# A layer-norm and MLP kernel: two DMA queues at the start, split transposes, and a new order of block 0's products

## The chip, the cores and the metric

The kernel runs on one core of a Trainium2 chip. The metric is the device time of one execution in microseconds (us). The "span" of a profile is the time from the first to the last instruction of one profiled execution; it is about 1.8 us shorter than that execution's time. PE is the matrix engine (TensorE), DVE is VectorE, ACT is ScalarE, POOL is GpSimd, SP is SyncE, and PEld is PE's loading of weights.

## The reference, cut to what matters

```python
# x: (1, 2048, 1024), w1: (1024, 3584), w2: (3584, 1024), all bf16
y = (x - mean(x)) / sqrt(var(x) + 1e-5)     # per row of 1024
h = gelu(y @ w1 + b1)                       # tanh approximation
out = h @ w2 + b2
```

## The kernel before

The 2048 rows of x are 16 tiles of 128 rows; 4 tiles make a block, so there are 4 blocks. For each block, PE computes the "first product" (`y @ w1`, 28 column blocks called `ft`, each a sum over 8 slices) and then the "second product" (`h @ w2`). All weights stay in SBUF after one load. In blocks 1 to 3 the first product takes all 4 tiles at once, 512 columns per matmul. In block 0 the data is still arriving, so it is cut into rectangles of tiles and `ft`:

```python
# (block, first tile, number of tiles, first ft, last ft)
rects.append((0, 0, 1, 0, lead_ft))                 # tile 0 alone, ft 0..3  (128 columns)
for i in range(1, NH):
    rects.append((0, i, 1, 0, lead_ft))             # tile 1 alone, ft 0..3
rects.append((0, 0, NH, lead_ft, KF))               # tiles 0 and 1, ft 4..27 (256 columns)
rects.append((0, NH, TPB - NH, 0, KF))              # tiles 2 and 3, ft 0..27 (256 columns)
```

The prologue of block 0: SyncE issues all loads in this order.

```python
for t in blocks[0][:NH]:
    load_x(t)                       # tile 0 in two halves, then tile 1
sp.dma_start(b1_raw[:], ...)        # b1
load_w1(0)                          # w1 chunk 0: ft 0..3, 1 MB
load_w1(1)
for t in blocks[0][NH:]:
    load_x(t)                       # tiles 2 and 3
for ci in range(2, NW1C):
    load_w1(ci)
# ... b2, the next block's x, w2, the rest of x
```

VectorE takes statistics of a tile (`st`, twice; `ag`; `ve`), POOL computes 1/sqrt, VectorE normalises (`nm`). PE then transposes the tile in 8 steps, and ScalarE and VectorE each copy half of the result from PSUM to `yT_sb` (`ET`), after all 8 steps. Until then PE runs 16 "warm-up" matmuls on zeros, and it transposes b1 before tile 0:

```python
pe_ops = [("warm", i) for i in range(n_warm)] + [("b1T",)]
pe_ops.append(("T", blocks[0][0]))
...
elif kind == "ET":                                   # on ScalarE
    a.wait_ge(sem_pe, pe_cnt[("T", t)])
```

So the first product needs two things: its weights (w1 chunk 0) and `yT` of tile 0.

Of the kernel before, what the change touches and what calls it, by code (L numbers as in the profile page):

```python
# [10 lines left out]
P = 128  # L11
LN_EPS = 1e-5
BANK = 512
# [10 lines left out]
def _mixer_mlp(nc, x, w1, b1, w2, b2, out, cfg):  # L24
# [7 lines left out]
    TPB = min(cfg.get("tiles_per_block", 4), TT)  # L32
    assert TT % TPB == 0
# [6 lines left out]
    CH = D // NCH  # L40
    W1C = min(cfg.get("w1_chunk", 512), F)
    assert F % W1C == 0 and W1C % P == 0
    NW1C = F // W1C
    FPC = W1C // P
    W2C = min(cfg.get("w2_chunk", 4), KF)
    assert KF % W2C == 0
    NW2C = KF // W2C
    NP1 = cfg.get("p1_banks", 3)
    NP2 = cfg.get("p2_banks", 2)
    NTB = cfg.get("t_banks", 2)  # L50
    assert NP1 + NP2 + NTB + 1 <= 8
    assert KD * P * 2 <= BANK * 4
    n_warm = cfg.get("n_warm", 0)
    tail_split = list(cfg.get("tail_split", [DBS]))
    dma_t = cfg.get("dma_transpose", True) and NB > 1
    lead = cfg.get("lead", True) and TPB >= 2
    lead_ft = min(cfg.get("lead_ft", FPC), KF)
    t1_after = cfg.get("t1_after", 2)
    t_first = cfg.get("t_first", 6)
    t_gap = cfg.get("t_gap", 3)  # L60
    KH = KD // 2 if KD >= 2 else KD
# [7 lines left out]
    NH = min(2, TPB)  # L69

    rects = []
    if lead:
        rects.append((0, 0, 1, 0, lead_ft))
        for i in range(1, NH):
            rects.append((0, i, 1, 0, lead_ft))
        if lead_ft < KF:
            rects.append((0, 0, NH, lead_ft, KF))
    else:
        rects.append((0, 0, NH, 0, KF))
    if TPB > NH:  # L80
        rects.append((0, NH, TPB - NH, 0, KF))
# [10 lines left out]
    def p2_ranges(t):  # L92
# [3 lines left out]
        assert sum(tail_split) == DBS  # L96
# [7 lines left out]
    pe_T_tiles = list(blocks[0]) if dma_t else list(range(TT))  # L104
    split_tiles = set(blocks[0]) if KH < KD else set()

    pe_ops = [("warm", i) for i in range(n_warm)] + [("b1T",)]
    pe_ops.append(("T", blocks[0][0]))
    pend_T = list(blocks[0][1:])
    if not lead:  # L110
        for _ in range(NH - 1):
            pe_ops.append(("T", pend_T.pop(0)))
    for ri in range(first_late_rect):
# [5 lines left out]
        for k, ft in enumerate(range(f0, f1)):  # L119
            pe_ops.append(("P1", ri, ft))  # L120
            done = k + 1
            if lead and ri == 0 and done == min(t1_after, f1 - f0):
                for _ in range(NH - 1):
                    pe_ops.append(("T", pend_T.pop(0)))
            if wide and i0 == 0 and pend_T and done >= t_first and (done - t_first) % t_gap == 0:
                pe_ops.append(("T", pend_T.pop(0)))
# [4 lines left out]
    for b in range(NB):  # L131
# [4 lines left out]
        nxt = list(blocks[b + 1]) if (b + 1 < NB and not dma_t) else []  # L136
        groups = [(t, o, w) for t in blocks[b] for (o, w) in p2_ranges(t)]
        stride = max(1, len(groups) // TPB)
        for gi, (t, o, w) in enumerate(groups):
            pe_ops.append(("P2", t, o, w))  # L140
            if nxt and gi % stride == 0:
                pe_ops.append(("T", nxt.pop(0)))
        for t in nxt:
            pe_ops.append(("T", t))
# [3 lines left out]
    t_seq = [op for op in pe_ops if op[0] == "T"]  # L148
# [8 lines left out]
    rot = {"early": 0, "late": 0}  # L157
    for (_, t) in t_seq:
        early = t in split_tiles
        pool = (T_BANKS + P2_BANKS) if early else T_BANKS  # L160
        key = "early" if early else "late"
        parts = []
        pieces = [(0, KH, "act"), (KH, KD, "dve")] if t in split_tiles else [(0, KD, "act")]
# [493 lines left out]
```

## Time and profile before

| | |
|---|---|
| time, median of 16 runs | 402.16 us (401.51 to 404.93) |
| span of the profiled run | 400.4 us |
| PE busy | 395.7 us, 99% |
| first product starts | 8.94 us |
| w1 chunk 0 complete | 8.80 us |
| yT of tile 0 ready | 8.34 us |
| second product of block 0 starts | 59.64 us |

The page of the profile opens with the span; its part 1 gives the busy time of each engine, its part 4 the chain of work that ended last.

```profile
span 400.4 us, 4765 instructions
PE 395.7 (99%) x2153; PEld 204.7 (51%) x2153; DVE 57.2 (14%) x120; ACT 89.0 (22%) x150; POOL 10.4 (3%) x23
PE 97%; DMA 2%; SPq 0%; issue 0%; DVE 0%
```

PE bounds the kernel and hardly ever waits. Only the time before its first product and the length of its matmul stream can be won. The same chain in order of time (start, length, what) shows both; L585 is the first product, L563 the transposes, L606 the second product.

```profile
1.70 0.42 SPq L341
2.16 0.46 SPq L359
2.67 6.13 DMA w_sb<-in_w_dram
...
8.94 1.05 PE ps L585 x16
...
18.80 1.75 PE ps L585 x16
20.55 0.06 issue
20.61 1.03 PE ps L585 x8
...
22.09 37.55 PE ps L585 x344
59.64 48.35 PE ps L606 x224
```

The issue of x tile 1 (L341) and of b1 (L359) stand before that of w1 chunk 0, whose data is complete at 8.80. At 20.55 there is a small wait. The timeline (start, length, engine, line, operation) shows the other chain, to `yT` of tile 0.

```profile
1.23 5.81 PE L547 MATMUL ps<-zero_sb 128*128 128x512 bf16 x16 [1.23 <-DVE zero_sb L441]
5.52 0.55 DVE L463 TENSOR_SCALAR x_sb<-x_sb,mv,rstd 128x1024 bf16<-128x1024 bf16 x1
7.09 0.62 PE L563 MATMUL ps<-ident,x_sb 128*128 128x128 bf16 x8
7.74 0.60 ACT L510 ACTIVATE yT_sb<-ps 128x512 bf16<-128x512 bf16 x1 [5.47 <-PE ps L563]
7.75 0.42 DVE L474 COPY yT_sb<-ps 128x512 bf16<-128x512 bf16 x1 [0.65 <-PE ps L563]
```

Tile 0 is normalised at 6.07, but the warm-ups hold PE until 7.04. Both copies are done at 8.34, still before the weights. In the view by windows (the last two columns are the share and the rate of the DMA engines, in GB/s) there is a hole in the stream of loads:

```profile
4.00:4.50 0.50, 0.50 (x2) 0.15 (x1) 0.47 (x2) 0.00 (x0) 0.00 (x0) 1.00 0.48 111
4.50:5.00 0.50, 0.50 (x2) 0.15 (x1) 0.47 (x3) 0.00 (x0) 0.07 (x1) 1.00 0.67 137
5.00:5.50 0.50, 0.50 (x3) 0.18 (x2) 0.40 (x1) 0.00 (x0) 0.49 (x1) 1.00 0.99 340
```

Last, the matmuls of the first product by form (count | busy us, mean ns):

```profile
L585 PE MATMUL ps<-yT_sb,w_sb 128*128 128x512 bf16 x672 | 145.5, 379 | 0.0
L585 PE MATMUL ps<-yT_sb,w_sb 128*128 128x256 bf16 x416 | 46.1, 273 | 0.1
```

Matmuls overlap, so the mean of one (273 or 379 ns) is longer than the spacing of the stream, and the rate is read from the chain: 37.55 us / 344 = 109.2 ns per matmul of 256 columns, 48.35 / 224 = 215.8 ns per matmul of 512.

### The profile page before, as it was taken

The page shows a single profiled execution, that of the slowest core. Times are in us where ns is not written, and L with a number is a line of the kernel's source. Part 1 is how long each engine was busy: PE and PEld are TensorE (multiplying, and loading weights), DVE is VectorE, ACT ScalarE, POOL GpSimd, SP SyncE. Part 2 cuts the span into 40 slices and gives each one's busy share as a digit, 9 for nine tenths or more (in the row PEclk, how much of TensorE's full clock was granted, in tenths as well). Part 3 has the DMA queues.
Part 4 walks back from the last instruction along what each step waited for, and adds up shares of the span by engine and source line. Part 5 has one row for each costly group of instructions (what it writes and reads, how often), then busy time and mean ns, then how long its engine had stood idle before and what let it go on. Part 6 is the DMA issues. An engine that isn't in the chain of part 4 may idle for free.

```text
span 400.4 us, 4765 instructions
## 1 busy us (share of the span) xinstructions
PE 395.7 (99%) x2153; PEld 204.7 (51%) x2153; DVE 57.2 (14%) x120; ACT 89.0 (22%) x150; POOL 10.4 (3%) x23
## 2 busy tenths in 40 slices
PE   7999999999999999999999999999999999999997
PEld 3988884444444444444444444444444444444446
DVE  5506100101260000101153000001100000001101
ACT  2655550000034442000013444100003344400000
POOL 1102000000020000000011000000000000000000
PEclk9999999999999999999999999999999999999999
DMA  7999964000014000000003200000000000000000
GB/s 244 354 362 387 386 213 82 26 26 28 21 34 78 0 0 2 5 22 28 26 28 62 43 2 0 0 28 26 0 28 26 2 0 0 2 0 26 28 26 28
DMA packets 29038, 26.79 MB, mean 67 GB/s; under 512 B 13786, under 2 KB 21466, under 8 KB 29018
## 3 DMA queue, kind: packets, MB, share of 16 engines
q1 hardware_dynamic: 29018, 26.49, 21.0%
q8 instruction: 17, 0.28, 0.3%
q14 instruction: 3, 0.02, 0.0%
HBM read 19.14 MB, written 4.19 MB: 58 GB/s over the span
## 4 chain that ended last, share of the span: by engine, by line
PE 97%; DMA 2%; SPq 0%; issue 0%; DVE 0%
PE ps L585 49%; PE ps L606 48%; DMA w_sb<-in_w_dram 2%; PE ps L563 0%; SPq L335 0%; SPq L359 0%; SPq L341 0%; DVE x_sb L484 0%
## 5 line engine op out<-in xcount | busy, mean ns | idle before, releaser
L585 PE MATMUL ps<-yT_sb,w_sb 128*128 128x512 bf16 (+2 forms) x1152 | 195.3, 332 | 1.3 <-DMA w_sb<-in_w_dram 1.2
L606 PE MATMUL ps<-w_sb,hT_sb 128*128 128x512 bf16 (+2 forms) x952 | 194.2, 366 | 0.0
L585 PEld LDWEIGHTS ps<-yT_sb,w_sb 128*128 128x128 bf16 x1152 | 109.8, 98 | 85.6 <-ACT yT_sb L510 1.4
L606 PEld LDWEIGHTS ps<-w_sb,hT_sb 128*128 128x128 bf16 x952 | 90.9, 98 | 102.7
L522 ACT ACTIVATE hT_sb<-ps,b_sb 128x512 bf16<-128x512 f32 (+2 forms) x144 | 85.2, 592 | 255.1 <-PE ps L585 254.8
L484 DVE TENSOR_TENSOR x_sb<-ps,b_bc 128x512 bf16<-128x512 f32 (+2 forms) x34 | 22.4, 660 | 318.3 <-PE ps L606 318.3
L449 DVE BATCH_NORM_STATS2 stats<-x_sb 128x6 f32<-128x512 bf16 x32 | 20.6, 682 | 13.7 <-DMA x_sb<-in_x_dram 13.7
L426 POOL TENSOR_TENSOR rstd<-veps,nhalf 128x1 f32<-128x1 f32 x16 | 9.7, 607 | 201.8 <-DVE veps L457 201.8
L463 DVE TENSOR_SCALAR x_sb<-x_sb,mv,rstd 128x1024 bf16<-128x1024 bf16 x16 | 7.9, 540 | 0.6 <-POOL rstd L426 0.4
L547 PE MATMUL ps<-zero_sb 128*128 128x512 bf16 x16 | 5.8, 544 | 1.2 <-DVE zero_sb L441 1.2
L547 PEld LDWEIGHTS ps<-zero_sb 128*128 128x128 bf16 x16 | 2.0, 133 | 4.5 <-issue 2.9
L510 ACT ACTIVATE yT_sb<-ps 128x512 bf16<-128x512 bf16 x4 | 2.4, 597 | 5.6 <-PE ps L563 5.5
L453 DVE BATCH_NORM_AGGREGATE mv<-stats 128x2 f32<-128x12 f32 x16 | 3.3, 209 | 0.6
L474 DVE COPY yT_sb<-ps 128x512 bf16<-128x512 bf16 x4 | 1.7, 424 | 6.8 <-PE ps L563 6.8
L457 DVE TENSOR_SCALAR veps<-mv 128x1 f32<-128x1 f32 x16 | 2.5, 154 | 0.6
L563 PE MATMUL ps<-ident,x_sb 128*128 128x128 bf16 x32 | 2.5, 219 | 0.0
L563 PEld LDWEIGHTS ps<-ident,x_sb 128*128 128x128 bf16 x32 | 2.0, 98 | 0.1
L503 ACT ACT_TABLE_LOAD x1 | 1.3, 1283 | 0.8 <-PEq L642 0.8
L441 DVE MEMSET zero_sb<- 128x256 uint32 x1 | 0.3, 272 | 0.9 <-PEq L642 0.9
L554 PEld LDWEIGHTS ps<-ident,b_raw 28*128 28x128 bf16 x1 | 0.1, 91 | 0.4 <-issue 0.4
L416 POOL TENSOR_SCALAR_AFFINE_SELECT ident<-ones_sb 128x128 bf16<-128x128 bf16 x1 | 0.3, 292 | 0.1
L413 POOL MEMSET ones_sb<- 128x128 bf16 x1 | 0.2, 204 | 0.3 <-POOLq L642 0.3
(8 smaller groups left out, 1.1 us busy)
## 6 DMA issues: line engine op xcount, KB each, us to landing
w_sb<-in_w_dram SPq DMA_DIRECT2D x14, 1024.0 KB, 13.4
x_sb<-in_x_dram SPq DMA_DIRECT2D x15, 256.0 KB, 8.7
out_dram<-x_sb SPq DMA_DIRECT2D x15, 256.0 KB, 2.0
x_sb<-in_x_dram SPq DMA_DIRECT2D x2, 128.0 KB, 2.3
b_bc<-in_b_dram SPq DMA_DIRECT2D x1, 256.0 KB, 9.5
yT_sb<-x_sb SPq DMA_TRANSPOSE x12, 3.1
out_dram<-x_sb SPq DMA_DIRECT2D x1, 128.0 KB, 1.7
out_dram<-x_sb SPq DMA_DIRECT2D x1, 64.0 KB, 2.7
```

The costliest lines, as they stand in the source:

```text
L426: ins = g.tensor_tensor(out=rstd[:, t:t + 1], in0=veps[:, t:t + 1], in1=nhalf[:], op=ALU.pow)
L449: ins = v.bn_stats(out=stats[:, t, ch, :], in_=x_sb[:, t, ch * CH:(ch + 1) * CH])
L453: ins = v.bn_aggr(out=mv[:, t, :], in_=stats[:, t, :, :].rearrange("p a b -> p (a b)"))
L457: ins = v.tensor_scalar(out=veps[:, t:t + 1], in0=mv[:, t, 1:2], scalar1=LN_EPS, scalar2=None, op0=ALU.add)
L463: ins = v.tensor_scalar(out=x_sb[:, t, :], in0=x_sb[:, t, :], scalar1=mv[:, t, 0:1], scalar2=rstd[:, t:t + 1], op0=ALU.subtract, op1=ALU.mult,
L484: ins = v.tensor_tensor(out=x_sb[:, t, o:o + w], in0=p2_bank(gi % NP2)[:, 0:w], in1=b2_bc[:, o:o + w], op=ALU.add,)
L510: ins = a.activation(out=yT_sb[:, slot, k0:k1, col:col + P], in_=t_part_ap(part).rearrange("p (k n) -> p k n", k=k1 - k0), func=ACTF.Copy,)
L522: ins = a.activation(out=hT_sb[:, ft, i0 * P:(i0 + nt) * P], in_=p1_bank(gi % NP1)[:, 0:nt * P], func=ACTF.Gelu_apprx_tanh, bias=b1_sb[:, ...
L547: ins = pe.matmul(p2_bank(op[1] % NP2), lhsT=zero_sb[:, 0:P], rhs=zero_sb[:], start=True, stop=True,)
L563: ins = pe.transpose(out=t_part_ap(part)[:, (kd - k0) * P:(kd - k0 + 1) * P], in_=x_sb[:, t, kd * P:(kd + 1) * P], identity=ident[:],)
L585: ins = pe.matmul(p1_bank(gi % NP1)[:, 0:nt * P], lhsT=w1_sb[:, kd, ft * P:(ft + 1) * P], rhs=yT_sb[:, slot, kd, i0 * P:(i0 + nt) * P], st ...
L606: ins = pe.matmul(p2_bank(gi % NP2)[:, 0:w], lhsT=hT_sb[:, kf, i * P:(i + 1) * P], rhs=w2_sb[:, kf, o:o + w], start=(kf == 0), stop=(kf == ...
```

## The change

Its intent: get the first product started earlier, and keep PE fed afterwards. It has three parts.

- **D, DMA.** b1 and x tile 1 are issued on ScalarE's queue; on SyncE, w1 chunk 0 follows x tile 0 at once.
- **C, prologue on the engines.** 12 warm-ups instead of 16. b1's transpose comes after tile 0's. 8 small "fill" matmuls follow. Each transpose is two operations of 4 steps (`Ta`, `Tb`), so ScalarE's copy starts after the first.
- **R, order of the products.** Tiles 0 and 1 together only up to `ft` 11, then tiles 2 and 3 up to 11, then all four with 512 columns. Tiles 2 and 3 are transposed earlier, and VectorE's order is adapted.

The diff cut to its core; removed options of the old configuration, renamings and the moved load functions are left out.

```diff
+PAIR_FT = 12
-    t_first = cfg.get("t_first", 6)          # steps before tile 2's transposes
-    t_gap = cfg.get("t_gap", 3)
+T_FIRST = 4
+T_GAP = 2
@@ rects
-            rects.append((0, 0, NH, lead_ft, KF))
-        rects.append((0, NH, TPB - NH, 0, KF))
+        rects.append((0, 0, NH, lead_ft, pair_ft))
+        rects.append((0, NH, TPB - NH, 0, pair_ft))
+            rects.append((0, 0, TPB, pair_ft, KF))
@@ PE's order
-    pe_ops = [("warm", i) for i in range(n_warm)] + [("b1T",)]     # n_warm = 16
-    pe_ops.append(("T", blocks[0][0]))
+    pe_ops = [("warm", i) for i in range(N_WARM)]                  # N_WARM = 12
+    pe_ops.append(("T", blocks[0][0]))
+    pe_ops.append(("b1T",))
+    pe_ops += [("fill", i) for i in range(N_FILL)]                 # N_FILL = 8
...
+    pe_ops = [h for op in pe_ops for h in ([("Ta", op[1]), ("Tb", op[1])] if op[0] == "T" else [op])]
@@ SyncE
-            for t in blocks[0][:NH]:
-                load_x(t)
-            sp.dma_start(b1_raw[:], ...)
-            load_w1(0)
+            load_x(sp, blocks[0][0])
+            load_w1(sp, 0)
@@ ScalarE
+            a.wait_ge(sem_pool, pool_cnt[("ones",)])
+            load_b1(a)
+            load_x(a, blocks[0][1])
...
-                    a.wait_ge(sem_pe, pe_cnt[("T", t)])
+                    a.wait_ge(sem_pe, pe_cnt[("Ta", t)])
```

More of the change, by code (lines that the diff above doesn't have):

```diff
@@ L11 @@
 P = 128
+BANK = 512
 LN_EPS = 1e-5
-BANK = 512
+TILES_PER_BLOCK = 4
+W1_CHUNK_FT = 4
+W2_CHUNK_KT = 4
+NP1 = 3
+NP2 = 2
+NTB = 2
+N_WARM = 12
+N_FILL = 8
+LEAD_FT = 4
+T1_AFTER = 2
+T_FIRST = 4
+T_GAP = 2
+X_AFTER = 2
+PAIR_FT = 12
+TAIL_SPLIT = (256, 128, 128)
 def _number(ops):
@@ L21, in _number, with _mixer_mlp @@
     return res
-def _mixer_mlp(nc, x, w1, b1, w2, b2, out, cfg):
+def _mixer_mlp(nc, x, w1, b1, w2, b2, out):
     xf = x.rearrange("b s d -> (b s) d")
@@ L30, in _mixer_mlp @@
     TT, KD, KF = S // P, D // P, F // P
-    TPB = min(cfg.get("tiles_per_block", 4), TT)
-    assert TT % TPB == 0
+    TPB = min(TILES_PER_BLOCK, TT)
+    assert TT % TPB == 0 and TPB >= 2
     NB = TT // TPB
@@ L40, in _mixer_mlp @@
     CH = D // NCH
-    W1C = min(cfg.get("w1_chunk", 512), F)
-    assert F % W1C == 0 and W1C % P == 0
-    NW1C = F // W1C
-    FPC = W1C // P
-    W2C = min(cfg.get("w2_chunk", 4), KF)
+    assert KD >= 2 and KD * P * 2 <= BANK * 4
+    assert NP1 + NP2 + NTB + 1 <= 8
+    KH = KD // 2
+    NH = 2
+    w1_bounds = [(f0, min(KF, f0 + W1_CHUNK_FT)) for f0 in range(0, KF, W1_CHUNK_FT)]
+    NW1C = len(w1_bounds)
+    w1_chunk_of = {ft: ci for ci, (f0, f1) in enumerate(w1_bounds) for ft in range(f0, f1)}
+    W2C = min(W2_CHUNK_KT, KF)
     assert KF % W2C == 0
     NW2C = KF // W2C
-    NP1 = cfg.get("p1_banks", 3)
-    NP2 = cfg.get("p2_banks", 2)
-    NTB = cfg.get("t_banks", 2)
-    assert NP1 + NP2 + NTB + 1 <= 8
-    assert KD * P * 2 <= BANK * 4
-    n_warm = cfg.get("n_warm", 0)
-    tail_split = list(cfg.get("tail_split", [DBS]))
-    dma_t = cfg.get("dma_transpose", True) and NB > 1
-    lead = cfg.get("lead", True) and TPB >= 2
-    lead_ft = min(cfg.get("lead_ft", FPC), KF)
-    t1_after = cfg.get("t1_after", 2)
-    t_first = cfg.get("t_first", 6)
-    t_gap = cfg.get("t_gap", 3)
-    KH = KD // 2 if KD >= 2 else KD
+    lead_ft = min(LEAD_FT, KF)
+    tail_split = list(TAIL_SPLIT) if sum(TAIL_SPLIT) == DBS else [DBS]
     xv = xf.rearrange("(t p) d -> p t d", p=P)
@@ L68, in _mixer_mlp @@
     blocks = [list(range(b * TPB, (b + 1) * TPB)) for b in range(NB)]
-    NH = min(2, TPB)
-    rects = []
-    if lead:
-        rects.append((0, 0, 1, 0, lead_ft))
-        for i in range(1, NH):
-            rects.append((0, i, 1, 0, lead_ft))
-        if lead_ft < KF:
-            rects.append((0, 0, NH, lead_ft, KF))
-    else:
-        rects.append((0, 0, NH, 0, KF))
+    dma_t = NB > 1
+    pair_ft = KF if TPB <= NH else max(lead_ft, min(PAIR_FT, KF))
+    rects = [(0, 0, 1, 0, lead_ft), (0, 1, 1, 0, lead_ft)]
+    if lead_ft < pair_ft:
+        rects.append((0, 0, NH, lead_ft, pair_ft))
     if TPB > NH:
-        rects.append((0, NH, TPB - NH, 0, KF))
+        rects.append((0, NH, TPB - NH, 0, pair_ft))
+        if pair_ft < KF:
+            rects.append((0, 0, TPB, pair_ft, KF))
     first_late_rect = len(rects)
@@ L95, in p2_ranges @@
             return base
-        assert sum(tail_split) == DBS
         last_o = base[-1][0]
@@ L102, in p2_ranges @@
         return res
-    pe_T_tiles = list(blocks[0]) if dma_t else list(range(TT))
-    split_tiles = set(blocks[0]) if KH < KD else set()
-    pe_ops = [("warm", i) for i in range(n_warm)] + [("b1T",)]
+    split_tiles = set(blocks[0])
+    pe_ops = [("warm", i) for i in range(N_WARM)]
     pe_ops.append(("T", blocks[0][0]))
+    pe_ops.append(("b1T",))
+    pe_ops += [("fill", i) for i in range(N_FILL)]
     pend_T = list(blocks[0][1:])
-    if not lead:
-        for _ in range(NH - 1):
-            pe_ops.append(("T", pend_T.pop(0)))
     for ri in range(first_late_rect):
@@ L121, in _mixer_mlp @@
             done = k + 1
-            if lead and ri == 0 and done == min(t1_after, f1 - f0):
+            if ri == 0 and done == min(T1_AFTER, f1 - f0):
                 for _ in range(NH - 1):
                     pe_ops.append(("T", pend_T.pop(0)))
-            if wide and i0 == 0 and pend_T and done >= t_first and (done - t_first) % t_gap == 0:
+            if wide and i0 == 0 and pend_T and done >= T_FIRST and (done - T_FIRST) % T_GAP == 0:
                 pe_ops.append(("T", pend_T.pop(0)))
@@ L135, in _mixer_mlp @@
                 pe_ops.append(("P1", ri, ft))
-        nxt = list(blocks[b + 1]) if (b + 1 < NB and not dma_t) else []
-        groups = [(t, o, w) for t in blocks[b] for (o, w) in p2_ranges(t)]
-        stride = max(1, len(groups) // TPB)
-        for gi, (t, o, w) in enumerate(groups):
-            pe_ops.append(("P2", t, o, w))
-            if nxt and gi % stride == 0:
-                pe_ops.append(("T", nxt.pop(0)))
-        for t in nxt:
-            pe_ops.append(("T", t))
+        for t in blocks[b]:
+            for (o, w) in p2_ranges(t):
+                pe_ops.append(("P2", t, o, w))
+    pe_ops = [h for op in pe_ops for h in ([("Ta", op[1]), ("Tb", op[1])] if op[0] == "T" else [op])]
     p1_seq = [op for op in pe_ops if op[0] == "P1"]
     p2_seq = [op for op in pe_ops if op[0] == "P2"]
-    t_seq = [op for op in pe_ops if op[0] == "T"]
+    t_seq = [("T", op[1]) for op in pe_ops if op[0] == "Ta"]
     p1_idx = {op: i for i, op in enumerate(p1_seq)}
@@ L156, in _mixer_mlp @@
     bank_user = {}
-    rot = {"early": 0, "late": 0}
+    rot = 0
+    pool_banks = T_BANKS + P2_BANKS
     for (_, t) in t_seq:
-        early = t in split_tiles
-        pool = (T_BANKS + P2_BANKS) if early else T_BANKS
-        key = "early" if early else "late"
         parts = []
-        pieces = [(0, KH, "act"), (KH, KD, "dve")] if t in split_tiles else [(0, KD, "act")]
-        for (k0, k1, eng) in pieces:
-            bank = pool[rot[key] % len(pool)]
-            rot[key] += 1
+        for (k0, k1, eng) in [(0, KH, "act"), (KH, KD, "dve")]:
+            bank = pool_banks[rot % len(pool_banks)]
+            rot += 1
             parts.append((bank, k0, k1, eng))
@@ L174, in _mixer_mlp @@
     for op in pe_ops:
-        if op[0] == "T":
+        if op[0] == "Ta":
             act_ops.append(("ET", op[1]))
@@ L183, in _mixer_mlp @@
     dve_ops = [("zero",)]
-    t0 = blocks[0][0]
-    if lead and NH > 1:
-        t1 = blocks[0][1]
-        h1 = ln_head(t1)
-        dve_ops += ln_head(t0) + h1[:1] + [("nm", t0)] + h1[1:]
-        dve_ops += [("ET", t0)] if t0 in split_tiles else []
-        dve_ops += [("b1c",), ("nm", t1)]
-        dve_ops += [("ET", t1)] if t1 in split_tiles else []
-        rest = blocks[0][2:]
-    else:
-        first = blocks[0][:NH]
-        for t in first:
-            dve_ops += ln_head(t)
-        for t in first:
-            dve_ops.append(("nm", t))
-        dve_ops.append(("b1c",))
-        for t in first:
-            if t in split_tiles:
-                dve_ops.append(("ET", t))
-        rest = blocks[0][NH:]
-    for t in rest:
-        dve_ops += ln_head(t)
+    t0, t1 = blocks[0][0], blocks[0][1]
+    h1 = ln_head(t1)
+    dve_ops += ln_head(t0) + h1[:1] + [("nm", t0)] + h1[1:]
+    dve_ops += [("ET", t0), ("b1c",), ("nm", t1), ("ET", t1)]
+    rest = blocks[0][2:]
+    prev = None
+    for t in rest:
+        h = ln_head(t)
+        if prev is None:
+            dve_ops += h
+        else:
+            dve_ops += h[:1] + [("nm", prev)] + h[1:]
+        prev = t
+    if prev is not None:
+        dve_ops.append(("nm", prev))
     for t in rest:
-        dve_ops.append(("nm", t))
-    for t in rest:
-        if t in split_tiles:
-            dve_ops.append(("ET", t))
+        dve_ops.append(("ET", t))
     for b in range(NB):
@@ L234, in _mixer_mlp @@
         if t == TT - 1 and len(rs) > D // DBS:
-            out_dmas[t] = [(t, o, w, ("E2", t, o, w)) for (o, w) in rs]
+            out_dmas[t] = [(o, w, ("E2", t, o, w)) for (o, w) in rs]
         else:
-            out_dmas[t] = [(t, 0, D, ("E2", t) + rs[-1])]
+            out_dmas[t] = [(0, D, ("E2", t) + rs[-1])]
     dmat_tiles = [t for b in range(1, NB) for t in blocks[b]] if dma_t else []
@@ L324, in wait_yT, with note, load_x @@
             eng.wait_ge(sem_act, act_cnt[("ET", t)])
-            if t in split_tiles:
-                eng.wait_ge(sem_dve, dve_cnt[("ET", t)])
+            eng.wait_ge(sem_dve, dve_cnt[("ET", t)])
+        loads = {}
+        def note(sm, val):
+            loads[sm.name] = (sm, val)
+        def load_x(eng, t):
+            if t == blocks[0][0]:
+                for ch in range(NCH):
+                    eng.dma_start(
+                        x_sb[:, t, ch * CH:(ch + 1) * CH], xv[:, t, ch * CH:(ch + 1) * CH]
+                    ).then_inc(sem_x0[ch], 16)
+                    note(sem_x0[ch], 16)
+                return
+            (sm, val), = x_waits(t, 0)
+            eng.dma_start(x_sb[:, t, :], xv[:, t, :]).then_inc(sm, 16)
+            note(sm, val)
@@ new lines, in load_b1, with load_b2, load_w1 @@
+        def load_b1(eng):
+            eng.dma_start(b1_raw[:], b1.rearrange("(k p) -> k p", p=P)).then_inc(sem_b1, 16)
+            note(sem_b1, 16)
+        def load_b2(eng):
+            eng.dma_start(
+                b2_bc[:], b2.rearrange("(o d) -> o d", o=1).broadcast_to([P, D])
+            ).then_inc(sem_b2, 16)
+            note(sem_b2, 16)
+        def load_w1(eng, ci):
+            f0, f1 = w1_bounds[ci]
+            eng.dma_start(w1_sb[:, :, f0 * P:f1 * P], w1v[:, :, f0 * P:f1 * P]).then_inc(sem_w1[ci], 16)
+            note(sem_w1[ci], 16)
@@ L328, in _, with load_w2 @@
+        def load_w2(eng, ci):
+            eng.dma_start(
+                w2_sb[:, ci * W2C:(ci + 1) * W2C, :], w2v[:, ci * W2C:(ci + 1) * W2C, :]
+            ).then_inc(sem_w2[ci], 16)
+            note(sem_w2[ci], 16)
         @block.sync
         def _(sp):
-            issued = []
-            def load_x(t):
-                if t == blocks[0][0]:
-                    for ch in range(NCH):
-                        sp.dma_start(
-                            x_sb[:, t, ch * CH:(ch + 1) * CH], xv[:, t, ch * CH:(ch + 1) * CH]
-                        ).then_inc(sem_x0[ch], 16)
-                        issued.append((sem_x0[ch], 16))
-                    return
-                (s, val), = x_waits(t, 0)
-                sp.dma_start(x_sb[:, t, :], xv[:, t, :]).then_inc(s, 16)
-                if (s, val) not in issued:
-                    issued.append((s, val))
@@ L345, in load_w1 @@
-            def load_w1(ci):
-                sp.dma_start(
-                    w1_sb[:, :, ci * W1C:(ci + 1) * W1C], w1v[:, :, ci * W1C:(ci + 1) * W1C]
-                ).then_inc(sem_w1[ci], 16)
-                issued.append((sem_w1[ci], 16))
-            def load_w2(ci):
-                sp.dma_start(
-                    w2_sb[:, ci * W2C:(ci + 1) * W2C, :], w2v[:, ci * W2C:(ci + 1) * W2C, :]
-                ).then_inc(sem_w2[ci], 16)
-                issued.append((sem_w2[ci], 16))
-            for t in blocks[0][:NH]:
-                load_x(t)
@@ L359, in _ @@
-            sp.dma_start(b1_raw[:], b1.rearrange("(k p) -> k p", p=P)).then_inc(sem_b1, 16)
-            issued.append((sem_b1, 16))
-            load_w1(0)
-            if NW1C > 1:
-                load_w1(1)
-            for t in blocks[0][NH:]:
-                load_x(t)
-            for ci in range(2, NW1C):
-                load_w1(ci)
-            sp.dma_start(
-                b2_bc[:], b2.rearrange("(o d) -> o d", o=1).broadcast_to([P, D])
-            ).then_inc(sem_b2, 16)
-            issued.append((sem_b2, 16))
+            load_x(sp, blocks[0][0])
@@ L372, in _ @@
+            load_w1(sp, 0)
+            nx = min(NW1C, max(1, X_AFTER))
+            for ci in range(1, nx):
+                load_w1(sp, ci)
+            for t in blocks[0][NH:]:
+                load_x(sp, t)
+            for ci in range(nx, NW1C):
+                load_w1(sp, ci)
+            load_b2(sp)
             if NB > 1:
                 for t in blocks[1]:
-                    load_x(t)
+                    load_x(sp, t)
             for ci in range(NW2C):
-                load_w2(ci)
+                load_w2(sp, ci)
@@ L377, in _ @@
             for b in range(2, NB):
                 for t in blocks[b]:
-                    load_x(t)
-            n_out = 0
-            def transposes(b):
-                for (s, val) in issued:
-                    sp.wait_ge(s, val)
-                del issued[:]
-                if n_out:
-                    sp.wait_ge(sem_out, 16 * n_out)
+                    load_x(sp, t)
+            note(sem_b1, 16)
+            for (sm, val) in x_waits(blocks[0][1], 0):
+                note(sm, val)
@@ L389, in transposes @@
+            state = {"loads_pending": True, "n_out": 0}
+            def transposes(b):
+                if state["loads_pending"]:
+                    for name in sorted(loads):
+                        sm, val = loads[name]
+                        sp.wait_ge(sm, val)
+                    state["loads_pending"] = False
+                if state["n_out"]:
+                    sp.wait_ge(sem_out, 16 * state["n_out"])
                 for t in blocks[b]:
@@ L400, in _ @@
                 for t in blocks[b]:
-                    for (_, o, w, e2) in out_dmas[t]:
+                    for (o, w, e2) in out_dmas[t]:
                         sp.wait_ge(sem_dve, dve_cnt[e2])
                         sp.dma_start(ov[:, t, o:o + w], x_sb[:, t, o:o + w]).then_inc(sem_out, 16)
-                        n_out += 1
-            sp.wait_ge(sem_out, 16 * n_out)
+                        state["n_out"] += 1
+            sp.wait_ge(sem_out, 16 * state["n_out"])
         @block.gpsimd
@@ L446, in _ @@
                     _, t, ch = op
-                    for (s, val) in x_waits(t, ch):
-                        v.wait_ge(s, val)
+                    for (sm, val) in x_waits(t, ch):
+                        v.wait_ge(sm, val)
                     ins = v.bn_stats(out=stats[:, t, ch, :], in_=x_sb[:, t, ch * CH:(ch + 1) * CH])
@@ L472, in _ @@
                     slot, col = tile_slot_col(t)
-                    v.wait_ge(sem_pe, pe_cnt[("T", t)])
+                    v.wait_ge(sem_pe, pe_cnt[("Tb", t)])
                     ins = v.tensor_copy(
@@ L550, in _ @@
                     )
+                elif kind == "fill":
+                    ins = pe.matmul(
+                        p1_bank(NP1 - 1)[:, 0:P], lhsT=zero_sb[:, 0:P], rhs=zero_sb[:, 0:P],
+                        start=True, stop=True,
+                    )
                 elif kind == "b1T":
@@ L554, in _ @@
                     ins = pe.transpose(out=ps_b1, in_=b1_raw[:], identity=ident[0:KF, 0:KF])
-                elif kind == "T":
+                elif kind in ("Ta", "Tb"):
                     t = op[1]
-                    for tp in t_prev[t]:
-                        wait_yT(pe, tp)
-                    pe.wait_ge(sem_dve, dve_cnt[("nm", t)])
-                    for part in t_parts[t]:
-                        _, k0, k1, _ = part
-                        for kd in range(k0, k1):
-                            ins = pe.transpose(
-                                out=t_part_ap(part)[:, (kd - k0) * P:(kd - k0 + 1) * P],
-                                in_=x_sb[:, t, kd * P:(kd + 1) * P],
-                                identity=ident[:],
-                            )
+                    if kind == "Ta":
+                        for tp in t_prev[t]:
+                            wait_yT(pe, tp)
+                        pe.wait_ge(sem_dve, dve_cnt[("nm", t)])
+                    part = t_part_of(t, "act" if kind == "Ta" else "dve")
+                    _, k0, k1, _ = part
+                    for kd in range(k0, k1):
+                        ins = pe.transpose(
+                            out=t_part_ap(part)[:, (kd - k0) * P:(kd - k0 + 1) * P],
+                            in_=x_sb[:, t, kd * P:(kd + 1) * P],
+                            identity=ident[:],
+                        )
                 elif kind == "P1":
@@ L579, in _ @@
                             wait_yT(pe, t)
-                    ci = (ft * P) // W1C
+                    ci = w1_chunk_of[ft]
                     if ci not in w1_seen:
@@ L627, in bass_standalone__mixer_channel_mlp__prompt_kernel @@
 ):
-    _mixer_mlp(nc, x, w1, b1, w2, b2, out, {"n_warm": 16, "tail_split": [256, 128, 128]})
+    _mixer_mlp(nc, x, w1, b1, w2, b2, out)
 _INS = ['x', 'w1', 'b1', 'w2', 'b2']
```

## The prediction

> **What bounds the kernel now.** TensorE: the page has PE busy 395.7 of 400.4 us, and the chain of waits puts 97% of the span on it. The chain is unbroken from 8.94 us, when the first real matmul starts, to 398.22. The granted clock is 1.00. So the change can win only (a) time before the first product, (b) matmul time after it.
>
> **(a) Prologue.** The chain there is five DMA issues on SyncE in a row (x tile 0 in two halves, x tile 1, b1, and w1 chunk 0 at 2.67), 0.40 to 0.46 us each, then 6.13 us until the chunk lands at 8.80. Behind it a second chain ends at 8.34: x tile 0 lands near 3.5, is normalised by 6.07, then PE is still busy with 16 warm-ups until 7.04, then transposes and two evictions. The change
> - issues w1 chunk 0 right after x tile 0, 0.97 us earlier (x tile 1 and b1 go to ScalarE's queue). The Trainium skill ("DMA: Bandwidth & Descriptors", "Issuing engines are not separate DMA queues") says a second queue saves only issue time; the same 1.58 MB must land. But DMA moved 111 and 137 GB/s in the two half-microseconds after 4.0, against 340 to 390 afterwards: a hole that x tile 1 can fill. I expect the chunk at 7.8.
> - takes away 4 warm-ups, puts b1's transpose behind x's, and starts the first eviction after 4 transposes: yT ready about 7.2, hidden behind the chunk. The 8 small fills only keep PE busy.
> So the first product starts near 7.9: 1.0 us won.
>
> **(b) Matmuls.** 256 of the 416 matmuls with 256 columns become 128 with 512. From the chain, 344 took 37.55 us (109.2 ns each), 224 took 48.35 (215.8 each). This agrees with the Trainium skill ("TensorE: Matmul & The Clock Gate", "Back-to-back issue gap": N/2.4+2.5). Saved: 128 x (2 x 109.2 - 215.8) = 0.3 us, all on the chain.
>
> Before, w1 chunk 3 landed at 20.47, just as PE asked for it (a gap of 0.06 us). An earlier start with the old order would meet that wait again. The new order (two tiles to block 12, the other two, then all four) asks for it only near 31 us, so the start isn't given back. Tiles 2 and 3 are asked for near 16 and 18 us; their normalisation ended at 16.31 and 17.30, and the new order brings it forward by about 1 us.
>
> The rest is unchanged.
>
> **Sum.** 1.0 + 0.3 + 0.06 = 1.4 us: from 402.1 to **400.7 us**; range 399.9 to 401.5. Chances: faster by over 2% 0.005, within 2% 0.99, slower by over 2% 0.005.
>
> **What would show each step.** First 128-column matmul at 7.9 (7.3 to 8.5) instead of 8.94, still released by w1's DMA; w1 issued at 1.7; 160 matmuls with 256 columns, 800 of the first product with 512; no PE wait for w1 or yT between 8 and 60 us.
>
> **What would make it wrong.** x tile 1 shares the engines with the chunk, which then lands little earlier (gain 0.4). x tile 1 landing after 5 us would stall VectorE, whose order puts its statistics before tile 0's normalisation: then yT is the bound. A table load ahead of ScalarE's DMA issues (1.28 us) would do that. Fewer warm-ups could leave the first products at half clock (64 matmuls of 65 ns: up to 4 us). Tile 3's transpose could wait on VectorE in the shorter pair phase. The before runs spread over 0.9 us, nearly the size of the effect.

## The result, and the profile after

| | before | after |
|---|---|---|
| time, median | 402.16 us (16 runs) | 400.84 us (11 runs, 400.47 to 401.35) |
| span of the profiled run | 400.4 | 399.6 |
| first product starts | 8.94 | 8.64 |
| second product of block 0 starts | 59.64 | 58.81 |

In this execution the first product starts above the prediction's range for it (7.3 to 8.5). The ratio is 0.996, with a 95% interval from 0.9944 to 0.9976. Ratios here are the mean time of one kernel's fast runs over that of the other's fast runs of the same rounds, so not quite the ratio of the medians. The change is small but clear of noise: 1.32 us between the medians. The profiled execution of the changed kernel, at 401.34 us, was one of its slowest, so it shows less of the gain.

Page and chain of the changed kernel (L591 is the first product, L569 the transposes, L612 the second product):

```profile
span 399.6 us, 4501 instructions
PE 395.2 (99%) x2029; PEld 192.3 (48%) x2029; DVE 57.2 (14%) x120; ACT 84.7 (21%) x134; POOL 10.3 (3%) x23
...
1.70 6.81 DMA w_sb<-in_w_dram
...
8.64 1.05 PE ps L591 x16
...
18.96 39.85 PE ps L591 x240
58.81 48.35 PE ps L612 x224
```

w1 chunk 0 is issued at 1.70 instead of 2.67, as intended, but it is complete only at 8.51, 0.29 earlier. The rest of the gain is in the stream: from the first to the second product 50.17 us instead of 50.70. The hole in the loads is gone (same windows view):

```profile
4.00:4.50 0.50, 0.50 (x2) 0.15 (x1) 0.47 (x2) 0.00 (x0) 0.00 (x0) 1.00 1.02 338
4.50:5.00 0.50, 0.50 (x2) 0.15 (x1) 0.22 (x2) 0.00 (x0) 0.09 (x1) 1.00 1.05 375
```

The timeline shows a stall that the prediction had named as a risk:

```profile
5.66 0.69 DVE L446 BATCH_NORM_STATS2 stats<-x_sb 128x6 f32<-128x512 bf16 x1 [0.91 <-DMA x_sb<-in_x_dram]
6.27 0.53 DVE L460 TENSOR_SCALAR x_sb<-x_sb,mv,rstd 128x1024 bf16<-128x1024 bf16 x1
6.86 0.62 PE L569 MATMUL ps<-ident,x_sb 128*128 128x128 bf16 x8 [0.41 <-DVE x_sb L460]
7.76 0.41 DVE L471 COPY yT_sb<-ps 128x512 bf16<-128x512 bf16 x1
```

VectorE waited 0.91 us for x tile 1, whose statistics stand before tile 0's normalisation in its order; `yT` was ready at 8.17. The trace also records each of the 16 shares in which a DMA lands. Fifteen shares of chunk 0 were in at 7.77 and the last at 8.51; of x tile 1, fifteen at 4.57 and the last at 5.64. The Trainium skill ("DMA: Bandwidth & Descriptors", section "Why a DMA increments its semaphore by 16 and not by 1") says why this counts: the shares finish independently, and only the full 16 mean that all data is there. This trace agrees: the first product started 0.14 us after the last share.

The matmuls of the first product by form:

```profile
L591 PE MATMUL ps<-yT_sb,w_sb 128*128 128x512 bf16 x800 | 173.3, 379 | 0.0
L591 PE MATMUL ps<-yT_sb,w_sb 128*128 128x256 bf16 x160 | 18.0, 273 | 0.0
```

### The profile page after: what moved, and what is told of

Read it like the earlier page. It is cut to its first block, busy times and chain, and to the rows that moved or that the text cites. A ratio compares the mean times of both kernels' runs of the same rounds, so it can differ in the third digit from the quotient of the medians.

```text
span 399.6 us, 4501 instructions
## 1 busy us (share of the span) xinstructions
PE 395.2 (99%) x2029; PEld 192.3 (48%) x2029; DVE 57.2 (14%) x120; ACT 84.7 (21%) x134; POOL 10.3 (3%) x23
## 3 DMA queue, kind: packets, MB, share of 16 engines
HBM read 19.14 MB, written 4.19 MB: 58 GB/s over the span
## 4 chain that ended last, share of the span: by engine, by line
PE 97%; DMA 2%; SPq 0%; issue 0%; DVE 0%
PE ps L591 49%; PE ps L612 48%; DMA w_sb<-in_w_dram 2%; PE ps L569 0%; SPq L321 0%; DVE x_sb L481 0%
## 5 line engine op out<-in xcount | busy, mean ns | idle before, releaser
L591 PE MATMUL ps<-yT_sb,w_sb 128*128 128x512 bf16 (+2 forms) x1024 | 194.8, 352 | 0.5 <-DMA w_sb<-in_w_dram 0.5
L612 PE MATMUL ps<-w_sb,hT_sb 128*128 128x512 bf16 (+2 forms) x952 | 194.2, 366 | 0.0
L591 PEld LDWEIGHTS ps<-yT_sb,w_sb 128*128 128x128 bf16 x1024 | 97.4, 98 | 96.6 <-issue 0.6
L612 PEld LDWEIGHTS ps<-w_sb,hT_sb 128*128 128x128 bf16 x952 | 90.9, 98 | 103.0
L522 ACT ACTIVATE hT_sb<-ps,b_sb 128x512 bf16<-128x512 f32 (+2 forms) x128 | 81.1, 634 | 259.1 <-PE ps L591 258.7
L569 PE MATMUL ps<-ident,x_sb 128*128 128x128 bf16 x32 | 2.5, 219 | 0.4 <-DVE x_sb L460 0.4
L569 PEld LDWEIGHTS ps<-ident,x_sb 128*128 128x128 bf16 x32 | 2.0, 98 | 1.3 <-DVE x_sb L460 1.2
```

What stands on the lines that cost most here:

```text
L522: ins = a.activation(out=hT_sb[:, ft, i0 * P:(i0 + nt) * P], in_=p1_bank(gi % NP1)[:, 0:nt * P], func=ACTF.Gelu_apprx_tanh, bias=b1_sb[:, ...
L569: ins = pe.transpose(out=t_part_ap(part)[:, (kd - k0) * P:(kd - k0 + 1) * P], in_=x_sb[:, t, kd * P:(kd + 1) * P], identity=ident[:],)
L591: ins = pe.matmul(p1_bank(gi % NP1)[:, 0:nt * P], lhsT=w1_sb[:, kd, ft * P:(ft + 1) * P], rhs=yT_sb[:, slot, kd, i0 * P:(i0 + nt) * P], st ...
L612: ins = pe.matmul(p2_bank(gi % NP2)[:, 0:w], lhsT=hT_sb[:, kf, i * P:(i + 1) * P], rhs=w2_sb[:, kf, o:o + w], start=(kf == 0), stop=(kf == ...
```

## The experiments

My theory: the first product starts when the later of two chains ends, that of the weights or that of `yT`; part D moves the first chain, part C the second, and R shortens what follows. The rivals: the parts simply add up; or all the gain is R's; or the late share is a property of the second queue.

The kernels with one or two parts were made by undoing the others in the changed kernel's source. By the traces, PE, VectorE and POOL of D alone, and SyncE and ScalarE of C alone, have their instructions in the order of the kernel before. A kernel with all three parts undone was not run. The twelve runs fell on three chips, four on each; the kernel before had medians of 402.10, 401.99 and 402.08 us there. Compare within a chip. Every start below is read from one profiled execution.

### First chip: the change again, and each part alone

**The changed kernel again** (e1_after_again), no edit.

> The changed kernel once more, unedited, to separate what is stable from what varies. In its first profile the first product began at 8.64 us because one of 16 DMA engines landed its share of w1 chunk 0 at 8.51 while the other 15 had landed by 7.77, and the same lateness showed in x tile 1 (5.64 against 4.58). Theory (a late engine is chance): in another execution the last share lands near 7.8 to 8.0, tile 1's near 4.6, and the first product starts at 7.9 to 8.3, span about 399.0. Rival (the second queue always makes one engine late): 8.5 to 8.6 again, span 399.6. Time in both: 1.0 to 1.6 us below the kernel before.

Measured: 400.91 us, ratio 0.9972 (0.996 to 0.9985), 1.2 us below before. Chunk 0 was complete at 8.09, its first share at 7.24; x tile 1 at 4.82; the first product started at 8.22, and the second 50.17 us later. The span was 399.2. So the late share was not a fixed property of the second queue. Nor does it need one: in C alone (below), where SyncE issues everything, fifteen shares of chunk 0 were in at 8.12 and the last at 8.97.

**Only D** (e2_dma_only).

```diff
 # the changed kernel with C and R undone
-N_WARM = 12
-N_FILL = 8
-PAIR_FT = 12
-T_FIRST = 4
-T_GAP = 2
+N_WARM = 16
+N_FILL = 0
+PAIR_FT = 28
+T_FIRST = 6
+T_GAP = 3
 # and: b1T ahead of T, ScalarE's copy waits for Tb, tiles 2 and 3 normalised after both statistics
```

> Only the DMA part (x tile 1 and b1 on ScalarE's queue, w1 chunk 0 issued second); prologue arithmetic and order of the products as before. Theory (two chains end in the first product, the later one counts): chunk 0 lands at 7.8 to 8.5, but 16 warm-ups keep PE until 7.04 and yT is ready only at about 8.3, so the product starts at 8.4 to 8.6: 0.3 to 0.5 us won, part of which may be given back at w1 chunk 3. Rival (gains add up): the product starts as soon as the chunk lands, 1.0 us won. Rival (nothing to be won in the prologue): 0.

Measured: 401.14 us, ratio 0.9983 (0.997 to 0.9997), 1.0 us below before: a miss of mine. Chunk 0 was complete at 8.00 and the product started at 8.13. `yT` was ready at 7.93, not 8.3, because in this execution the 16 warm-ups ended at about 6.6 and not 7.04 (see the four warm-ups below). D alone yields the larger part of the gain (0.7 us by the ratio, 1.0 by the medians, against 1.1 to 1.2 for the whole change), but the intervals of the two overlap. The `yT` chain ended only 0.07 us before the weights, so this run does not part my theory from the rival that gains add up: the product started with the chunk. The runs that do are those below in which `yT` came last. The same chain in order of time:

```profile
1.70 6.29 DMA w_sb<-in_w_dram
...
8.13 1.05 PE ps L591 x16
```

**Only C** (e3_compute_only).

```diff
 # the changed kernel with D and R undone (R as above)
-            load_w1(sp, 0)
+            load_x(sp, blocks[0][1])
+            load_b1(sp)
+            load_w1(sp, 0)
@@ ScalarE
-            load_b1(a)
-            load_x(a, blocks[0][1])
```

> Only the prologue arithmetic (12 warm-ups, b1's transpose after tile 0's, 8 fills, first eviction released after 4 transposes); DMA issues and order of the products as before. Theory: yT ready at 7.2 to 7.5 instead of 8.34, but w1 chunk 0 still lands at 8.8, so the product starts at 8.9 and the time is that of before within 0.2 us. Rival (the gain comes from the warm-ups and the split transposes): start 0.5 us or more earlier.

Measured: 401.89 us, ratio 0.9997 (0.9984 to 1.001): no gain, as the theory has it. The timeline of this run:

```profile
6.85 0.41 DVE L473 COPY yT_sb<-ps 128x512 bf16<-128x512 bf16 x1
...
9.10 0.61 PE L590 MATMUL ps<-yT_sb,w_sb 128*128 128x128 bf16 x8 [1.85 <-DMA w_sb<-in_w_dram]
```

`yT` was ready at 7.26, a whole microsecond earlier than before, and PE then waited 1.85 us for the weights. The rival that credits warm-ups and split transposes by themselves falls.

**Only R** (e4_order_only).

```diff
 # the changed kernel with D and C undone; what remains of the change:
-T_FIRST = 6
-T_GAP = 3
-PAIR_FT = 28
+T_FIRST = 4
+T_GAP = 2
+PAIR_FT = 12
@@ VectorE's order for tiles 2 and 3
-            dve_ops += h
+            dve_ops += h[:1] + [("nm", prev)] + h[1:]
```

> Only the order of block 0's products (two tiles to block 12, the other two to block 12, then all four; transposes of tiles 2 and 3 and their VectorE order to match); prologue and DMA as before. Theory: start unchanged at 8.9; from there to the start of the second product 50.2 us instead of 50.7 (0.3 us from 128 matmuls of 512 columns in place of 256 of 256, 0.2 us from the wait for w1 chunk 3 at 20.5), so 0.5 us faster. Rival (matmul width is worth nothing because PE is at its peak either way): 0.2 us or less.

Measured: 401.45 us, ratio 0.9988 (0.9976 to 1.0001). The first product started at 8.65, 0.3 earlier than expected (chunk 0 was complete at 8.52 by the luck of this execution), and the second 50.17 us later. In the two runs above with the old order it was 50.49 us. So R is worth 0.32 us in the stream, in line with 128 x (2 x 109.2 - 215.8) = 0.33 us.

### Second chip: D with C, and what the first product waits for

**D and C, without R** (e5_dma_and_compute; the edit is `PAIR_FT = 28`, `T_FIRST = 6`, `T_GAP = 3` and VectorE's old order for tiles 2 and 3).

> The changed kernel with the old order of block 0's products (the DMA and the arithmetic part together, two tiles at a time through all 28 blocks of w1). Theory: first product at 8.0 to 8.5 as in the whole change, then 50.5 us to the second product (50.2 with the new order), and a wait for w1 chunk 3 of 0 to 0.3 us at about 20 us if its last share lands after 20 us; time 0.9 us below before, 0.3 to 0.5 above the whole change. Rival (an early start is given back entirely at chunk 3): no faster than before less 0.3.

Measured: 401.51 us, ratio 0.9987 (0.9975 to 0.9999), 0.5 us below before. The first product started at 8.50 (chunk 0 complete at 8.37) and the second 50.49 us later. There was no wait at w1 chunk 3, here or with D alone: the chunk landed at 19.33 us here and at 19.44 with D alone, earlier with the rest of the stream. In the profile of before it had landed at 20.47, and in that of R alone, with the same issue order, at 20.43. The wait seen there was not a barrier for an earlier start, though D alone had little to spare: by its distance from the first product, chunk 3 was due at about 19.7.

**Tile 1 behind chunk 0** (e6_tile1_behind_chunk0).

```diff
@@ VectorE
-    dve_ops += ln_head(t0) + h1[:1] + [("nm", t0)] + h1[1:]
-    dve_ops += [("ET", t0), ("b1c",), ("nm", t1), ("ET", t1)]
+    dve_ops += ln_head(t0) + [("nm", t0)] + h1[:1]
+    dve_ops += [("ET", t0), ("b1c",)] + h1[1:] + [("nm", t1), ("ET", t1)]
@@ SyncE
             load_w1(sp, 0)
+            load_x(sp, blocks[0][1])
@@ ScalarE
-            load_x(a, blocks[0][1])
```

> The changed kernel with x tile 1 issued on SyncE behind w1 chunk 0 instead of beside it on ScalarE's queue, and with VectorE's order changed so that tile 0's normalisation does not stand behind tile 1's statistics. Theory (chunk 0 is bound by the bytes that must land with it, at about 365 GB/s): 262 KB fewer ahead of it, so its last share lands 0.5 to 0.8 us earlier, near 7.4, and the first product starts at about 7.5; tile 1 lands near 8.2, its transposes come 1 to 2 us late and PE waits there, so the time is no better than the changed kernel's. Rival (chunk 0 is bound by its issue and its own transfer): it lands at 8.0 to 8.5 as before the edit.

Measured: 403.22 us, ratio 1.0038 (1.0024 to 1.0052), slower; the profiled run had a granted clock of 0.996, so only its first microseconds are used. Chunk 0 was complete at 7.08 against 8.37 and 7.89 in the other runs on this chip that have tile 1 beside it (the run above and the next one). This speaks for bytes: tile 1's 262 KB at about 365 GB/s are 0.72 us, and the first share of chunk 0 came 0.70 us earlier (6.46 against 7.15 and 7.16). The last share moved by 0.8 to 1.3 us, more than the bytes explain; what is over lies in how late the last share was in the other two. The first product nevertheless began only at 8.92, 0.10 us after `yT`, a miss of mine. I had left tile 1's first statistics ahead of tile 0's copy, and VectorE waited there for tile 1, as this chain shows:

```profile
2.17 5.61 DMA x_sb<-in_x_dram
...
7.80 0.69 DVE stats L447
8.49 0.32 DVE yT_sb L472
```

**Only VectorE's order** (e7_stats_later), the first hunk of the diff above.

> The changed kernel with only VectorE's order edited: tile 0's normalisation ahead of tile 1's first statistics, and tile 0's eviction and b1's copy ahead of the rest of tile 1's. Theory: yT of tile 0 is ready at 7.0 to 7.2 (7.35 in the second profile of the changed kernel, 8.17 in its first, where tile 1 came late), but the first product still waits for w1 chunk 0 until 8.0 to 8.5, so the time is that of the changed kernel within 0.2 us. Rival (VectorE's order sets the start): 0.4 us or more faster.

Measured: median 401.56 us (one run of six, at 403.82 with a granted clock of 0.996, pulls the ratio to 1.0001), 0.4 us below before. The changed kernel itself was not run on this chip, so my "within 0.2 us" of it cannot be checked. `yT` was ready at 7.22, but the product started at 8.03 with the weights (complete at 7.89): the rival falls. The edit also did harm. It put the rest of tile 1's statistics behind b1's copy, and PE then waited 0.6 us for tile 1's normalisation:

```profile
9.69 0.62 PE L569 MATMUL ps<-ident,x_sb 128*128 128x128 bf16 x8 [0.61 <-DVE x_sb L460]
```

**The same with chunk 0 cut in half**, that is, VectorE's order as in the last run and this (e8_half_chunk):

```diff
-X_AFTER = 2
+X_AFTER = 3
+    w1_bounds = [(0, 2), (2, 4)] + w1_bounds[1:]
```

> As e7_stats_later, and w1 chunk 0 cut into two halves of 512 KB, each with its own semaphore. Theory (the first product waits for bytes): 0.5 MB fewer have to land, 1.4 us at 365 GB/s, so the first half is there at 6.7 to 7.2, the first product starts at 7.1 to 7.4, now about equally bound by yT, and the time falls 0.6 to 1.0 us below the changed kernel's, to about 400.1. It may give back 0.1 to 0.3 us at w1 chunk 2, which lands near 15.6 and is asked for at 15.7. Rival (the last share is late because of one slow DMA engine, not because of the bytes): the start moves by 0.3 us or less.

Measured: 401.54 us, ratio 0.9988. The half chunk was complete at 6.84 and the first product started at 7.59, 0.10 us after `yT` (7.49): now the `yT` chain was the later one. But PE waited 1.3 us at the transposes of tile 1, which my order of VectorE had delayed. The gain in the start was real and was lost one step later, and my forecast of the time missed.

### Third chip: the half chunk cleanly, and the warm-ups

**Half a chunk, and nothing else** (e9_half_chunk_only: the last diff, on the changed kernel).

> The changed kernel with w1 chunk 0 cut into two halves and nothing else (VectorE's order left as the change has it, unlike e8_half_chunk, where tile 1's transposes waited 1.3 us for VectorE). Theory (first product waits for bytes, then for yT): the first half lands at 6.8 to 7.2, yT is ready at 7.4 to 8.2 depending on when tile 1 lands, so the first product starts at 7.5 to 8.3, at least 0.4 us earlier on average; tile 1's normalisation ends near 8.3, before its transposes are due (8.6), so nothing is given back there; a wait of up to 0.2 us at the next chunks. Time 0.4 to 0.8 us below e11_after_again of the same chip. Rival (tile 1 bounds again): a wait of PE for x of 0.3 us or more and no gain.

**The same, tuned** (e10_half_chunk_tuned): also `N_WARM = 10` and `T1_AFTER = 3`.

> As e9_half_chunk_only, with 10 warm-ups instead of 12 (they ended at 6.3 to 6.5 where tile 0 was normalised by 6.1) and tile 1's transposes after 3 steps of the first product instead of 2 (half a microsecond later, to let tile 1 be late). Theory: transposes of tile 0 begin at 6.1, yT ready at 7.2 to 7.4 when tile 1 is not late, first product at 7.4; no wait of PE for VectorE, but 0.1 us for tile 1's eviction; time 0 to 0.3 us below e9_half_chunk_only, 0.6 to 1.0 below e11_after_again. Rival (fewer warm-ups leave the clock low): the first 16 products take over 1.3 us instead of 1.05.

**The changed kernel, unedited, on this chip** (e11_after_again).

> The changed kernel unedited, on the chip of e9 and e10 for comparison, and a third look at where the first product starts: 8.0 to 8.6 us, released by w1 chunk 0; 1.0 to 1.4 us below the kernel before.

Measured: 400.86 us for the half chunk (0.9975), 400.66 tuned (0.9976), 400.82 for the changed kernel (0.9969, 0.9957 to 0.9981). The three are the same within the noise, so both forecasts of a gain missed. The chain of the half chunk shows why:

```profile
7.38 1.05 PE ps L592 x16
...
8.91 2.68 PE ps L592 x48
11.59 0.10 issue
11.69 3.65 PE ps L592 x32
15.34 0.05 issue
15.39 0.61 PE ps L570 x8
16.00 0.06 issue
16.06 1.91 PE ps L592 x16
...
58.26 48.35 PE ps L613 x224
```

And the changed kernel's on the same chip:

```profile
8.29 1.05 PE ps L591 x16
...
58.46 48.35 PE ps L612 x224
```

The first product starts 0.91 us earlier, and the second only 0.20 earlier: 50.88 us of stream instead of 50.17. The other 0.71 us came back in three waits. PE met the second w1 megabyte (complete at 11.55, next matmul at 11.69), then tile 2's normalisation (tile 2 landed at 12.23, and PE waited 0.3 us for its transposes), then the third megabyte (complete at 15.92, next matmul at 16.06). There the stream of loads sets the pace until 16 us. The changed kernel started at 8.29 and had no such wait: its third megabyte was complete at 15.53 and first used at 16.25.

The tuned version started at 7.72, later than the untuned one. With 10 warm-ups, the 8 transposes took 1.02 us instead of 0.62: PE was not yet at full rate. But they took 0.97 us in the run of D with C too, with 12 warm-ups, so this one execution does not show that the two were needed. The second product began at 58.23, as in the other two.

**Four warm-ups** (e12_four_warmups: `N_WARM = 4` on the changed kernel).

> The changed kernel with 4 warm-ups instead of 12, to measure the cost that the prediction named as a risk. Theory ([...]the warm-ups of before ran at 427 ns each until about 5.9 us and at 216 ns after): PE idles from 2.9 to 6.0 us, so transposes and the first products run at about twice their time, 107 ns instead of 65 per 128-column product, for 3 to 4 us: 1.5 to 2.5 us slower than the changed kernel. Rival (warm-ups are worth nothing): same as e11_after_again.

Measured: 401.95 us, ratio 1.0001: 1.1 us slower than the changed kernel, less than I expected. Its timeline:

```profile
1.24 1.89 PE L547 MATMUL ps<-zero_sb 128*128 128x512 bf16 x4 [1.24 <-DVE zero_sb L438]
6.36 1.04 PE L569 MATMUL ps<-ident,x_sb 128*128 128x128 bf16 x8 [3.24 <-DVE x_sb L460]
8.29 1.91 PE L591 MATMUL ps<-yT_sb,w_sb 128*128 128x128 bf16 x16
```

The transposes of tile 0, the fills and the first 16 products ran at about half rate; from the third of tile 1's transposes on, all ran at full rate. The first product waited for neither chain here (weights 7.88, `yT` 7.86) but for the 8 fills, which stand before it on PE. The Trainium skill ("TensorE: Matmul & The Clock Gate", section "Part 1: The HAM clock gate") states that PE runs at half rate until it has been busy for a window of about 3.4 us, and that this window is free-running. The runs agree in the main: 512-column warm-ups stand 427 ns apart first and 216 ns later, and the same 12 warm-ups took between 4.17 and 5.30 us in different executions. In the changed kernel's second profile the change came about 2.9 us after the first warm-up, sooner than a whole window; no run explains that. The varying moment fits the miss of my forecast for D alone, and the 0.97 us of transposes in the run with D and C, where all twelve warm-ups stood about 427 ns apart.

## Why the prediction was right, and where it was not

The predicted time, 400.7 us, came within 0.14 us of the measured 400.84. This is closer than the steps behind it were. Step by step:

1. **PE bounds the kernel, and only the start and the stream can be won: right.** The chain after the change has the same form.
2. **w1 chunk 0 is issued 0.97 us earlier: right** (1.70 instead of 2.67). **"I expect the chunk at 7.8": too early.** The last share came at 8.80, 8.97 and 8.52 us in the three profiles with the old issue order (mean 8.76), and at 8.51, 8.09, 8.16, 8.00, 8.37, 7.89 and 7.88 in the seven with tile 1 beside the chunk (mean 8.13); within the first chip, 8.97 and 8.52 against 8.09 and 8.00. That is 0.63 us of gain, not 1.0. The mis-sized term is the arrival: I moved it by the whole issue time. What was won is about what the hole held: (365 - 124) GB/s for 1 us are 241 KB, or 0.66 us at 365 GB/s. This is an estimate from the windows view, and it fits the 0.63. The Trainium skill's section "Issuing engines are not separate DMA queues" ("DMA: Bandwidth & Descriptors") says that a second queue saves only issue time; the estimate suggests that even the issue time counts only as far as the DMA engines were idle meanwhile.
3. **yT ready about 7.2 and hidden behind the weights: right in kind.** It was 7.35 and 7.58 in two profiles of the changed kernel. In the third it was 8.17, because x tile 1 landed after 5 us and stalled VectorE, as the prediction's list of risks had said. Even there the weights came later. C alone gained nothing. That the later chain decides is shown by all traces but one: in the nine in which the weights came last, the first product started 0.14 us after them, and in the four in which `yT` did (tile 1 behind chunk 0, and the three with half a chunk), 0.10 us after it. The exception is the run with four warm-ups.
4. **0.3 us from wider matmuls: right.** 50.49 us became 50.17. One qualification to the prediction's citation: that section calls N/2.4+2.5 the gap of an isolated matmul and gives about 131 ns for 512 columns in a stream. The stream here, at 215.8 ns, agrees with the formula and not with the 131.
5. **"An earlier start with the old order would meet that wait again": not confirmed.** D alone and D with C started 0.8 and 0.4 us earlier with the old order and met no wait. The wait in the profile of before, 0.22 us in all and not 0.06, came from a late landing of chunk 3: fifteen shares were in at 19.14, the last at 20.47. Three other executions with the old order of products had no such wait. The prediction also expected the normalisation of tiles 2 and 3 about 1 us earlier; tile 2's ended at 15.21 instead of 16.31, but tile 3's at 17.52 instead of 17.30. PE waited for neither.
6. **The sum.** The stream gives 0.32 us, and 0.53 against the execution profiled before. The start gives 0.63 from the landings. Together that is 0.95 to 1.16 us, where 1.2 to 1.3 were measured; the difference is within the noise and not explained. The spans tell the same over more executions: after is 391.0 us from first product to end in its three profiles, so its median span of 399.1 over 22 runs places the first product at 8.1. This is an estimate. For before, 400.3 less 391.3 to 391.5 gives 8.8 to 9.0. So the start was worth 0.6 to 0.9 us, where 1.0 was predicted. That the total nevertheless came so near to 1.4 is in part luck.

What stays open: why one of 16 shares is late in some executions. The traces do not say what delayed it. The pieces of C (fewer warm-ups, b1's transpose later, fills, split transposes) and of D (b1's issue, tile 1's issue) were not run one by one.

## What to carry to other kernels

When a start waits for two chains, measure both ends before shortening either: here shortening the `yT` chain alone gave nothing, and moving the weights alone gave the larger part of the gain. Count the bytes that must land before the first use, not only the position of its issue; here an earlier issue gained about what the DMA engines had been idle, and the next loads became the bound as soon as the first was out of the way. After an edit to one engine's order, look one step further down the chain: twice here a gain at tile 0 was paid back at tile 1.

## What the Trainium skill lacked or had wrong

- "DMA: Bandwidth & Descriptors": it says that the 16 shares finish independently, but not how far apart. Here the first and the last share of w1 chunk 0 (1 MB) landed 0.6 to 1.45 us apart (7.27 and 7.88 in one run, 7.52 and 8.97 in another), and a single share was up to 0.85 us behind the other fifteen. The first product started only after the last.
- "DMA: Bandwidth & Descriptors", "Issuing engines are not separate DMA queues": nothing wrong, but it calls the saved issue time usually small relative to the DMA. Here 0.97 us of issue time brought the load in 0.63 us earlier, and a prologue on the critical path pays for that.
- "TensorE: Matmul & The Clock Gate": its half rate at the start agrees (427 ns per 512 columns). The page warns that the clock-gate events of a trace can be unreliable; here is a case where the granted clock does not show the half rate at all. That column read 1.00 from 1 to 6 us while the warm-ups ran at 427 ns, and also in the run with four warm-ups. Only the spacing of the matmuls showed it.
